# A recurrent state with an MLP behind it on one core: the order of VectorE's first work, whole first tiles, and the place of the early weights

## The chip, the cores and the metric

The kernel runs on one core of one Trainium2 chip. Its engines are TensorE (PE: matmul; PEld is its weight load), VectorE (DVE), ScalarE (ACT), GpSimd (POOL) and SyncE (SP), which issues transfers; each works through its own queue in order. The metric is the device time of one execution in microseconds (us). The median of 3 runs of the kernel before is 829.57 us.

## The reference

```python
def _attn_ref(r, k, v, w, a, b):                 # 4 x 8 heads, 768 positions, 40 wide, float32
    ...
    for t in range(S):
        ...
        y[:, :, t] = np.einsum('bhd,bhde->bhe', rt, state)
        Sa = np.einsum('bhde,bhe->bhd', state, at)
        state_decay = state * wt[:, :, None, :] - np.einsum('bhd,bhe->bhde', Sa, bt)
        state = state_decay + np.einsum('bhd,bhe->bhde', vt, kt)
...
    h = x @ w_in                                  # 3072 x 320 by 320 x 2048
    sp = np.where(h > 20.0, h, np.log1p(np.exp(np.minimum(h, 20.0))))
    g = h * np.tanh(sp)
    return (g @ w_out).astype(np.float32)         # by 2048 x 320
```

A state of 40 x 40 per head runs through 768 positions; at each position it is decayed by w, reduced by a product with a and b, and raised by v and k. The outputs y, put side by side over the heads, go through an MLP.

## The kernel before

The 768 positions are cut into 12 chunks of 64 (`C`, `nch`). Within a chunk the recurrence is solved with matrices; from chunk to chunk only the state is carried. Chunks are handled in six pairs n = 0 to 5 (chunks 2n and 2n+1). The work of a pair has three parts.

`pre_a(c, be)` (from L126) is called four times for a pair: two chunks c, two halves be of the heads. It loads a tile `wa` (decays and a, L131) and a tile `bk` (b and k, L134), two transfers each because the 40 rows of two groups of heads go to partitions 0 to 39 and 64 to 103. The first call also loads `cst` (identity and masks) and fills a column block of `bk` from it (L138). On VectorE follow a reduce (L145), two reciprocals (L146, L156), a product scan `P` forward (L147) and one backward (L157), and products into `wa` (L152) and `bk` (L170). ACT copies the scaled a to `ad` (L155). TensorE multiplies `ad` and `bk` (L186), and ACT and VectorE write the results to `GP` (L188, L189, L193) and `HA` (L190, L191); TensorE transposes `bk` (L202). `wa` and `bk` have two buffers each (`NWA`), used in turns; `P` goes to memory (L172, on GpSimd's queue).

`pre_inv(n)` (from L205) inverts triangular 32 x 32 blocks of the whole pair on VectorE: a transpose `XL` (L209), thirty times a product `tmp` (L214) and an addition (L216), each needing the one before, and two transposes `TT` and `T1` (L218, L220). `post_inv(n)` takes these on TensorE (L232, L241, L258) and ACT (L235, L249 to L251, L260) to the tiles `KT`, one for each chunk and half.

`step(c)` (from L349) runs one chunk with its state: its matmuls are L284, L293, L304, L314, L334 and L339, VectorE masks the result (L316) and forms the new state `ST` (L342, L346), ACT copies (L286, L294, L343). Step c needs the `KT` of its chunk and the state after step c - 1. GpSimd's queue carries its loads (L267 to L271) and the store of y.

The MLP (from L550) runs over the 12 chunks with weights that are split into a high and a low part by `split` (L489): a transfer `cv_d` (L453, on SP), ACT (L459, L494) and four operations of VectorE (L461 to L463, L495). `M.early()` converts the first quarter of `w_in` in three pieces with one buffer for `cv_d`; the rest follows when the space of `pre_a` is free (`M.first`, `M.second`, `M.third`).

A planner orders the instructions: each engine's queue takes, in the planner's own model of time, the ready instruction of the best priority. Priority is the place in the program, and `at(tc, k)` moves a block ahead by `OFF[k]` places (L38, L44). The program's order is `pa(0)`, `inv(0)`, the four calls of pair 1, `M.early()`, and then for each n the letters of `ORDER`: step 2n, `pa(n+2)`, `inv(n+1)`, step 2n+1.

Of the kernel before, what the change touches and what calls it, by code (L numbers as in the profile page):

```python
# [33 lines left out]
NSTN = 1  # L34
LA = 2
ORDER = '0aiA1'

OFF = {'I': 80, 'T1': 80, 'P00': -40, 'P10': 80, 'P11': 40, 'b0': 15, 'c0': 600, 'u0': -15, 'u1': 250, 'd0': 250,  # L38
       'd1': 150, 'W': 600, 'V': 400, 'E': 150, 'I0': 600, 'I1': 300, 'I2': 300, 'I3': 300, 'I4': 300, 'p4': 15,
       'I5': 300, 'J5': 600, 's0': 150, 's2': -15, 's3': 80, 's4': 250, 's6': -15, 's7': -40, 's8': 150, 's10': -150}  # L40
SORD = 'a0 b0 u0 d0 a1 b1 u1 d1 c0 c1'

# [5 lines left out]
def layouts(inp, S=768):  # L48
    nch = S // C

    def v(x):
        return x[:, :, :S].reshape(4, 2, 2, 2, nch, C, 40)

    r, k, vv, w, a, b = (v(inp[n]) for n in 'rkvwab')
    o = {}
    wt = w.transpose(4, 2, 1, 6, 3, 0, 5).reshape(nch, 2, 2, 40, 8, C)
    wa = np.zeros(wt.shape[:4] + (1040,), np.float32)
    wa[..., :520].reshape(wt.shape[:4] + (8, 65))[..., 1:] = wt
    wa[..., 528:] = a.transpose(4, 2, 1, 6, 3, 0, 5).reshape(nch, 2, 2, 40, 512)
    o['wa'] = wa  # L60
    bt, kt = (x.transpose(4, 2, 1, 6, 3, 0, 5).reshape(nch, 2, 2, 40, 8, 1, C) for x in (b, k))
    bk = np.concatenate([bt, kt], -2)
    bk[:, 1] = np.concatenate([kt, bt], -2)[:, 1]
    o['bk'] = bk.reshape(nch, 2, 2, 40, 8, 128)
    o['rD'] = np.ascontiguousarray(r.transpose(4, 1, 6, 2, 3, 0, 5)).reshape(nch, 2, 40, 16, C)
    o['vD'] = np.ascontiguousarray(vv.transpose(4, 1, 6, 3, 0, 2, 5)).reshape(nch, 2, 40, 8, 128)
    o['vN'] = np.ascontiguousarray(vv.transpose(4, 2, 5, 3, 0, 1, 6)).reshape(nch, 2, C, 16, 40)
    p = np.arange(128)
    cst = np.zeros((128, 328), np.float32)
    cst[:, :128] = np.eye(128)  # L70
    cst[:, 128:192] = (p[:, None] % 64) < np.arange(64)
    cst[:, 192:256] = np.arange(64) < (p[:, None] // 64) * 32 + p[:, None] % 32
    cst[:, 256:296] = (p[:, None] % 64) == np.arange(40)
    cst[:, 296:328] = np.arange(32) < p[:, None] % 32
    o['cst'] = cst
    return o


def attention(ctx, tc, I, yD, pD, nch, M):
# [25 lines left out]
    bdT = [ci.tile([128, 8, 2, 64], F32, name=f"bdT{i}") for i in range(2)]  # L105
    z = cs.tile([128, 1], F32, name="z")
    V.memset(z, 0.0)
    for w, b in zip(wab, bkb):
        V.memset(w, 1.0)
        G.memset(b, 0.0)  # L110
    for t in [d1] + [x.rearrange("p s k a t -> p (s k a t)") for x in adb[:NAD]]:
        A.copy(t, z.broadcast_to(t.shape))
    for t in bdT:
# [6 lines left out]
    for t in VS + [UVT] + bdr[:NBR] + ST:  # L120
        G.memset(t, 0.0)

    RW, W2, HA, BKN, GP, KT = {}, {}, {}, {}, {}, {}
    LQ, SQ, OQ, PQ = (dict(S=SP, G=G, A=A)[x] for x in QS)

    def pre_a(c, be):  # L126
        n = 2 * c + be
        wa, bk, ad = wab[n % NWA], bkb[n % NWA], adb[n % 2]
        for al in range(2):
            q = slice(al * 64, al * 64 + 40)  # L130
            LQ.dma_start(out=wa[q], in_=I['wa'][c, be, al])  # L131
        for al in range(2):
            q = slice(al * 64, al * 64 + 40)
            LQ.dma_start(out=bk[q, :, 0:128], in_=I['bk'][c, be, al])  # L134
        if (c, be) == (0, 0):
            LQ.dma_start(out=cst, in_=I['cst'])
            for t in bkb:
                A.copy(t[:, :, 128:168], cst[:, 256:296].unsqueeze(1).broadcast_to([128, 8, 40]))  # L138
        wz, a = wa[:, 0:521], wa[:, 528:1040]
        P = pw.tile([128, 520], F32, name="P", bufs=NP)  # L140
        E = wa[:, 520:1040]
        w2 = pw.tile([128, 2, 8], F32, name="w2", bufs=4)
        wz3 = wz[:, 0:520].rearrange("p (s j) -> p s j", j=65)

        V.tensor_reduce(out=w2[:, 0], in_=wz3[:, :, 1:33], axis=AX.X, op=ALU.mult)  # L145
        V.reciprocal(d1[:, 64:584:65], w2[:, 0])  # L146
        V.tensor_tensor_scan(out=P, data0=wz[:, 0:520], data1=d1[:, 64:584], initial=0.0, op0=ALU.mult, op1=ALU.add)  # L147
        P3 = P.rearrange("p (s j) -> p s j", j=65)
        E3 = E.rearrange("p (s j) -> p s j", j=65)
        V.tensor_copy(w2[:, 1], P[:, 64:520:65])  # L150
        a3 = a.rearrange("p (s t) -> p s t", t=64)
        V.tensor_tensor(out=a3, in0=a3, in1=P3[:, :, 0:64], op=ALU.mult)  # L152
        for al in range(2):
            q = slice(al * 64, al * 64 + 64)
            A.copy(ad[q, :, :, al], a[q].rearrange("p (s k t) -> p s k t", k=2, t=32))  # L155
        V.reciprocal(d1[:, 64:584:65], w2[:, 1])  # L156
        V.tensor_tensor_scan(out=E[:, 0:519][:, ::-1], data0=wz[:, 2:521][:, ::-1], data1=d1[:, 1:520][:, ::-1],  # L157
                             initial=0.0, op0=ALU.mult, op1=ALU.add)
        W2[be] = w2
        if be == 1:  # L160

            RW[c] = wk.tile([128, 2, 16], F32, name="rw", bufs=4)
            pt = ps_g.tile([128, 2, 16], F32, name="pa")
            for b2 in range(2):
                for al in range(2):
                    PE.matmul(pt[b2 * 64:b2 * 64 + 64, al], ident[:, al * 64:al * 64 + 64], W2[b2].rearrange("p a b -> p (a b)"),
                              start=(al == 0), stop=True, skip_group_check=True)
            A.copy(RW[c], pt)
        bk4 = bk[:, :, 0:128].rearrange("p s (x t) -> p s x t", x=2)
        V.tensor_tensor(out=bk4, in0=bk4, in1=E3[:, :, 0:64].unsqueeze(2).broadcast_to([128, 8, 2, 64]), op=ALU.mult)  # L170
        for al in range(2):
            PQ.dma_start(out=pD[c, be, :, al], in_=P[al * 64:al * 64 + 40])  # L172

        if c % 2 == 0 and be == 0:
            GP[c // 2] = iw.tile([128, 32, 2, 32], F32, name="GP", bufs=NGP)
        gp = GP[c // 2]
        u0 = (c % 2) * 16 + be * 8
        ha = iw.tile([128, 8, 104], F32, name="HA", bufs=NHA)
        HA[c, be] = ha
        oa, oh = (0, 40) if be == 0 else (64, 0)  # L180
        og, ok = (0, 64) if be == 0 else (64, 0)
        for s0 in (0, 3, 6):
            m = min(3, 8 - s0)
            pt = ps_g.tile([128, 3, 168], F32, name="pa")
            for j in range(m):
                PE.matmul(pt[:, j], ad[:, s0 + j].rearrange("p k a t -> p (k a t)"), bk[:, s0 + j], start=(j == 0), stop=True,  # L186
                          skip_group_check=True)
            A.mul(gp[0:64, u0 + s0:u0 + s0 + m, 1], pt[0:64, 0:m, og:og + 32], -1.0)  # L188
            A.mul(gp[64:128, u0 + s0:u0 + s0 + m].rearrange("p u k i -> p u (k i)"), pt[64:128, 0:m, og:og + 64], -1.0)  # L189
            A.copy(ha[:, s0:s0 + m, oa:oa + 40], pt[:, 0:m, 128:168])  # L190
            V.tensor_tensor(out=ha[:, s0:s0 + m, oh:oh + 64], in0=pt[:, 0:m, ok:ok + 64],  # L191
                            in1=maskH.unsqueeze(1).broadcast_to([128, m, 64]), op=ALU.mult)
        V.tensor_tensor(out=gp[:, u0:u0 + 8, 1], in0=gp[:, u0:u0 + 8, 1], in1=maskG.unsqueeze(1).broadcast_to([128, 8, 32]),  # L193
                        op=ALU.mult)

        bkn = wk.tile([128, 664], F32, name="bkn", bufs=NBKN)
        BKN[c, be] = bkn
        G.memset(bkn[:, 640:664], 0.0)
        for s0 in (0, 4):
            pt = ps_g.tile([128, 4, 2, 64], F32, name="pa")  # L200
            for j in range(4):
                PE.transpose(pt[:, j].rearrange("p a b -> p (a b)"), bk[:, s0 + j, 0:128], ident)  # L202
            A.copy(bkn[:, s0 * 80:s0 * 80 + 320].rearrange("p (s a e) -> p s a e", a=2, e=40), pt[:, :, :, 0:40])

    def pre_inv(n):  # L205
# [11 lines left out]
        TT = iw.tile([128, 32, 32], F32, name="TT", bufs=NTT)  # L217
        V.transpose(TT.rearrange("p u t -> p t u"), X)  # L218
        T1 = gp[0:64, :, 0]
        V.transpose(T1, TT[0:64])  # L220
        return TT, T1

    def post_inv(n, TT, T1):
        gp = GP[n]
# [155 lines left out]

    def inv(n):
        with at(tc, 'I%d' % n), at(tc, 'I'):
            TT, T1 = pre_inv(n)
        with at(tc, 'J%d' % n):
            post_inv(n, TT, T1)

    pa(0)
    inv(0)
    for u in range(4):
        with at(tc, 'P%d%d' % (u // 2, u % 2)):  # L390
            pre_a(2 + u // 2, u % 2)
    for n in range(nds):
        if n + 1 == nds:
            ictx.close()
            with at(tc, 'V'):
                M.second()
        if n == 0:
            with at(tc, 'E'):
                M.early()
        for k in ORDER:  # L400
            if k in '01':
                step(2 * n + int(k))
            elif k == 'i':
                if n + 1 < nds:
                    inv(n + 1)
            elif k == 'a':
                pa(n + LA)
            elif k == 'A' and n + 2 == nds:
# [249 lines left out]
```

## Time and profile before

| | us |
|---|---|
| median of 3 runs | 829.57 (829.17 to 835.69) |
| profiled execution | 826.83 |
| its span | 825.1 |
| mean granted TensorE clock | 0.964 |

The profile is that of one execution; its span is counted from its first to its last instruction. A row of the timeline has the start, the length (us), the engine, the line, the operation, what it writes and reads with the shapes, the count, and in brackets the idle time of the engine before it with what ended it. A row of a group has a count, then the busy time in us, the mean of one in ns, and the idle time before. The rows themselves stand in the prediction.

### The profile page before, as it was taken

What the parts mean: (1) busy time and instruction counts of PE and PEld (TensorE: products, weight loads), DVE (VectorE), ACT (ScalarE), POOL (GpSimd) and SP (SyncE); (2) the same over time, 40 slices, a digit from 0 to 9 for tenths busy, and PEclk for the clock granted to TensorE, in tenths of its full rate; (3) what the DMA queues carried; (4) which work ended last, traced back from release to release, by engine and by line L of the source; (5) the groups of instructions that cost most, each with busy time, mean ns of one, the idle gap of its engine ahead of it and who ended that gap; (6) DMA issues with size and microseconds to landing.
All of it is one profiled execution on the core that took longest, in us unless ns stands there. A gap on an engine that the chain in (4) does not pass through costs nothing.

```text
span 825.1 us, 18795 instructions
## 1 busy us (share of the span) xinstructions
PE 724.1 (88%) x7816; PEld 679.3 (82%) x7816; DVE 461.1 (56%) x975; ACT 428.6 (52%) x937; POOL 103.2 (13%) x182
## 2 busy tenths in 40 slices
PE   2544798999789889889886999999999999999998
PEld 1433687788788788778775899999999999999998
DVE  6789979748989758889846456222222122122110
ACT  5534658775485866666784556233333333333331
POOL 8100021223222023221102100000000000000000
PEclk9767889999989999999999999999999999999999
DMA  6522323334433233423328543121121112000000
GB/s 174 143 73 65 96 54 73 93 82 111 106 84 81 60 97 103 92 74 111 105 92 191 130 139 99 39 56 33 23 55 37 36 39 55 18 20 17 17 1 33
DMA packets 58213, 61.92 MB, mean 75 GB/s; under 512 B 25536, under 2 KB 48704, under 8 KB 58128
## 3 DMA queue, kind: packets, MB, share of 16 engines
q1 hardware_dynamic: 49296, 40.94, 17.7%
q0 software_dynamic: 8832, 19.79, 9.9%
q8 instruction: 61, 1.00, 0.5%
q14 instruction: 24, 0.20, 0.1%
HBM read 48.79 MB, written 11.86 MB: 74 GB/s over the span
## 4 chain that ended last, share of the span: by engine, by line
PE 51%; ACT 9%; DVE 8%; DMA 4%; issue 2%; SPq 0%; DVEq 0%; ACTq 0%
PE ph L583 21%; PE po L604 7%; PE po L605 7%; PE po L603 7%; PE pa L258 3%; DMA cv_d<-in_wo 2%; PE pa L186 2%; DVE tmp L214 1%; DVE XL L216 1%; ACT bdT L249 1%; ACT bdT L250 1%; PE pq L314 1%; ACT KT L260 1%; PE pu L284 1%; DMA cv_d<-in_wi 1%
## 5 line engine op out<-in xcount | busy, mean ns | idle before, releaser
L583 PE MATMUL ph<-xh,w_ih 128*128 128x256 f32 x576 | 148.3, 283 | 3.1 <-ACT xh L566 3.1
L585 ACT ACTIVATE g<-ph 128x512 f32<-128x512 f32 x96 | 57.3, 598 | 180.0 <-PE ph L583 179.9
L589 DVE TENSOR_TENSOR gl<-g,gh 128x1024 fp32r<-128x1024 f32 x48 | 58.6, 1225 | 159.1 <-ACT gh L588 158.8
L583 PE MATMUL ph<-xh,w_il 128*128 128x256 f32 x576 | 123.7, 283 | 0.0
L186 PE MATMUL pa<-bk,ad 128*128 128x168 f32 x384 | 80.6, 359 | 45.5 <-DVE bk L170 15.0
L604 PE MATMUL po<-w_ol,gh 128*128 128x320 f32 x384 | 118.7, 309 | 0.1
L605 PE MATMUL po<-w_oh,gl 128*128 128x320 f32 x384 | 118.4, 309 | 0.0
L603 PE MATMUL po<-w_oh,gh 128*128 128x320 f32 x384 | 117.9, 309 | 0.0
L583 PEld LDWEIGHTS ph<-xh,w_ih 128*128 128x128 f32 x576 | 109.3, 190 | 3.4 <-ACT xh L566 3.4
L186 PEld LDWEIGHTS pa<-bk,ad 128*128 128x128 f32 x384 | 67.0, 222 | 50.8 <-issue 22.8
L583 PE MATMUL ph<-xl,w_ih 128*128 128x256 f32 x384 | 100.9, 284 | 0.0
L583 PEld LDWEIGHTS ph<-xh,w_il 128*128 128x128 f32 x576 | 96.2, 190 | 0.1
L583 PEld LDWEIGHTS ph<-xl,w_ih 128*128 128x128 f32 x384 | 73.1, 190 | 0.5 <-issue 0.3
L604 PEld LDWEIGHTS po<-w_ol,gh 128*128 128x128 f32 x384 | 72.1, 188 | 0.5 <-DVE w_ol L495 0.5
L605 PEld LDWEIGHTS po<-w_oh,gl 128*128 128x128 f32 x384 | 72.1, 188 | 0.1
L603 PEld LDWEIGHTS po<-w_oh,gh 128*128 128x128 f32 x384 | 71.8, 188 | 0.2
L216 DVE TENSOR_TENSOR XL<-XL,tmp 128x30 f32<-128x30 f32 (+9 forms) x180 | 59.0, 328 | 2.4
L214 DVE TENSOR_TENSOR tmp<-XL 128x30 f32<-128x30 f32 (+9 forms) x180 | 58.6, 325 | 2.3
L258 PE MATMUL pa<-bdT,HA 128*104 128x128 f32 x384 | 52.3, 291 | 6.9 <-ACT bdT L251 5.7
L258 PEld LDWEIGHTS pa<-bdT,HA 128*104 128x104 f32 x384 | 47.3, 182 | 10.6 <-ACT bdT L251 7.4
L314 PE MATMUL pq<-bdr,UVT 128*128 128x128 f32 x384 | 53.7, 285 | 0.3 <-DVE UVQ L316 0.2
L588 ACT CAST gh<-g 128x1024 fp32r<-128x1024 f32 x48 | 50.1, 1048 | 1.1
(89 smaller groups left out, 1219.6 us busy)
## 6 DMA issues: line engine op xcount, KB each, us to landing
wa<-in_wa SPq DMA_DIRECT2D x48, 162.5 KB
bk<-in_bk SPq DMA_DIRECT2D x48, 160.0 KB
cv_d<-in_wi SPq DMA_DIRECT2D x12, 512.0 KB
cv_d<-in_wo SPq DMA_DIRECT2D x8, 640.0 KB
pD<-P POOLq DMA_DIRECT2D x48, 81.2 KB, 2.2
VS<-in_vN POOLq DMA_DIRECT2D x24, 160.0 KB, 3.5
UVT<-in_vD POOLq DMA_DIRECT2D x24, 160.0 KB, 4.4
bdr<-in_rD POOLq DMA_DIRECT2D x24, 160.0 KB, 4.4
```

The costliest lines, as they stand in the source:

```text
L186: PE.matmul(pt[:, j], ad[:, s0 + j].rearrange("p k a t -> p (k a t)"), bk[:, s0 + j], start=(j == 0), stop=True, skip_group_check=True)
L214: V.tensor_tensor(out=tv, in0=X[:, i + 1:32, i:i + 1].broadcast_to([128, 31 - i, i]), in1=X[:, i:i + 1, 0:i].broadcast_to([128, 31 - i, i] ...
L216: V.tensor_tensor(out=X[:, i + 1:32, 0:i], in0=X[:, i + 1:32, 0:i], in1=tv, op=ALU.add)
L258: PE.matmul(pk[:, j], ha[:, s0 + j], bd[:, s0 + j].rearrange("p a t -> p (a t)"), start=(j == 0), stop=True, skip_group_check=True)
L314: PE.matmul(pq[:, s], UVT[:, g * 4 + s, be * 128:be * 128 + 128], br[:, be, g * 4 + s].rearrange("p a t -> p (a t)"), start=(s == 0), stop ...
L583: PE.matmul(o, w, x, start=(j == 0 and n == 0), stop=(n == 7), skip_group_check=True)
L585: A.activation(g[:, f0:f0 + 2], ph, AF.Mish)
L588: A.copy(gh, g)
L589: V.tensor_tensor(out=gl, in0=g, in1=gh.bitcast(F32), op=ALU.subtract)
L603: PE.matmul(po[k], gh[:, j, t], oh, start=(f == 0), stop=False, skip_group_check=True)
L604: PE.matmul(po[k], gh[:, j, t], ol, start=False, stop=False, skip_group_check=True)
L605: PE.matmul(po[k], gl[:, j, t], oh, start=False, stop=(f == 15), skip_group_check=True)
```

## The change

The change has four parts.

1. The calls of pair 1's `pre_a` are put under `tc.issue_after(ends[0])`, where `ends[0]` is the last transpose (`T1`) of inverse 0. This gives every VectorE instruction of those calls a place in VectorE's queue behind that transpose; it is an order within one queue and no semaphore. Their offset becomes 100 (key `F`) for all four; it was -40, 0, 80 and 40.
2. For n = 0 the order of the letters is `ORDER0`: step 0, inverse 1, step 1, then `pa(2)`. The other n keep `ORDER`.
3. For chunk 0 the host lays out whole tiles of 128 partitions, `wap` (ones where there is no data) and `bkp` (zeros, and the column block that L138 copied from `cst`). The two calls for chunk 0 load them with one transfer for `wa` and one for `bk`. The memsets of the `wa` and `bk` buffers (L109, L110) and ACT's copies (L138) go.
4. `M.early()` moves from n = 0 to n = 2 (`NE`). Its VectorE instructions are ordered behind the last transpose of inverse 1 (`ends[1]`), its transfers on SP behind the last `bk` load of pair 1 (`ld`).

```diff
+ORDER0 = '0i1a'
+NE = 2
...
+       'd1': 150, 'W': 600, 'V': 400, 'E': 150, 'I0': 600, 'I1': 300, 'F': 100, 'I2': 300, 'I3': 300, 'I4': 300, 'p4': 15,
...
+    wap = np.ones((2, 2, 64, 1040), np.float32)
+    wap[:, :, 0:40] = wa[0]
+    bkp = np.zeros((2, 2, 64, 8, 168), np.float32)
+    bkp[:, :, 0:40, :, 0:128] = o['bk'][0]
+    bkp[:, :, :, :, 128:168] = np.eye(64, 40, dtype=np.float32)[:, None]
+    o['wap'] = wap.reshape(2, 128, 1040)
+    o['bkp'] = bkp.reshape(2, 128, 1344)
...
-    for w, b in zip(wab, bkb):
-        V.memset(w, 1.0)
-        G.memset(b, 0.0)
...
+        if c == 0:
+            LQ.dma_start(out=wa, in_=I['wap'][be])
+            LQ.dma_start(out=bk.rearrange("p s t -> p (s t)"), in_=I['bkp'][be])
+        else:
...
+                last[0] = LQ.dma_start(out=bk[q, :, 0:128], in_=I['bk'][c, be, al]).ins
         if (c, be) == (0, 0):
             LQ.dma_start(out=cst, in_=I['cst'])
-            for t in bkb:
-                A.copy(t[:, :, 128:168], cst[:, 256:296].unsqueeze(1).broadcast_to([128, 8, 40]))
...
-        V.transpose(T1, TT[0:64])
-        return TT, T1
+        return TT, T1, V.transpose(T1, TT[0:64])
...
     pa(0)
-    inv(0)
+
+    ends = [inv(0)]
     for u in range(4):
-        with at(tc, 'P%d%d' % (u // 2, u % 2)):
+        with at(tc, 'F'), tc.issue_after(ends[0]):
             pre_a(2 + u // 2, u % 2)
+    ld = last[0]
     for n in range(nds):
...
-        if n == 0:
-            with at(tc, 'E'):
+        if n == NE:
+            with at(tc, 'E'), tc.issue_after(ends[1]), tc.issue_after(ld):
                 M.early()
-        for k in ORDER:
+        for k in ORDER if n else ORDER0:
...
-                    inv(n + 1)
+                    ends.append(inv(n + 1))
```

More of the change, by code (lines that the diff above doesn't have):

```diff
@@ L36 @@
 ORDER = '0aiA1'
+ORDER0 = '0i1a'
+NE = 2
 OFF = {'I': 80, 'T1': 80, 'P00': -40, 'P10': 80, 'P11': 40, 'b0': 15, 'c0': 600, 'u0': -15, 'u1': 250, 'd0': 250,
-       'd1': 150, 'W': 600, 'V': 400, 'E': 150, 'I0': 600, 'I1': 300, 'I2': 300, 'I3': 300, 'I4': 300, 'p4': 15,
+       'd1': 150, 'W': 600, 'V': 400, 'E': 150, 'I0': 600, 'I1': 300, 'F': 100, 'I2': 300, 'I3': 300, 'I4': 300, 'p4': 15,
        'I5': 300, 'J5': 600, 's0': 150, 's2': -15, 's3': 80, 's4': 250, 's6': -15, 's7': -40, 's8': 150, 's10': -150}
@@ L121, in attention @@
         G.memset(t, 0.0)
+    last = [None]
     RW, W2, HA, BKN, GP, KT = {}, {}, {}, {}, {}, {}
@@ L128, in pre_a @@
         wa, bk, ad = wab[n % NWA], bkb[n % NWA], adb[n % 2]
[L129 to L134, printed above, removed]
+        if c == 0:
+            LQ.dma_start(out=wa, in_=I['wap'][be])
+            LQ.dma_start(out=bk.rearrange("p s t -> p (s t)"), in_=I['bkp'][be])
+        else:
+            for al in range(2):
+                q = slice(al * 64, al * 64 + 40)
+                LQ.dma_start(out=wa[q], in_=I['wa'][c, be, al])
+            for al in range(2):
+                q = slice(al * 64, al * 64 + 40)
+                last[0] = LQ.dma_start(out=bk[q, :, 0:128], in_=I['bk'][c, be, al]).ins
         if (c, be) == (0, 0):
             LQ.dma_start(out=cst, in_=I['cst'])
-            for t in bkb:
-                A.copy(t[:, :, 128:168], cst[:, 256:296].unsqueeze(1).broadcast_to([128, 8, 40]))
         wz, a = wa[:, 0:521], wa[:, 528:1040]
@@ L382, in inv @@
         with at(tc, 'I%d' % n), at(tc, 'I'):
-            TT, T1 = pre_inv(n)
+            TT, T1, end = pre_inv(n)
         with at(tc, 'J%d' % n):
             post_inv(n, TT, T1)
+        return end.ins
     pa(0)
-    inv(0)
+    ends = [inv(0)]
     for u in range(4):
-        with at(tc, 'P%d%d' % (u // 2, u % 2)):
+        with at(tc, 'F'), tc.issue_after(ends[0]):
             pre_a(2 + u // 2, u % 2)
+    ld = last[0]
     for n in range(nds):
```

## The prediction

> **What bounds the kernel now.** I read the page first: the engines' rows and the 40 slices.
>
> ```profile
> PE 724.1 (88%) x7816; PEld 679.3 (82%) x7816; DVE 461.1 (56%) x975; ACT 428.6 (52%) x937; POOL 103.2 (13%) x182
> PE   2544798999789889889886999999999999999998
> DVE  6789979748989758889846456222222122122110
> ```
>
> TensorE (PE) is full from the 23rd slice on (22 x 20.6 = 454 us): that is the MLP. What a change at the beginning can win is how much earlier that stretch begins. TensorE's holes lie in the first five slices, where VectorE (DVE) carries the high digits. The windows view gives this by stage; its columns are stage, length, then busy us and instructions of PE, PEld, DVE, ACT, POOL, then granted clock, DMA share, GB/s:
>
> ```profile
> 0.00:25.00 25.00, 7.87 (x45) 7.00 (x45) 17.86 (x33) 12.80 (x29) 17.57 (x29) 1.00 0.67 170
> 25.00:50.00 25.00, 14.12 (x68) 11.82 (x68) 18.35 (x37) 12.98 (x38) 1.97 (x8) 0.73 0.37 113
> 48.00:97.00 49.00, 22.59 (x181) 18.04 (x180) 48.18 (x120) 21.73 (x63) 5.07 (x10) 0.79 0.24 71
> 97.00:147.00 50.00, 45.78 (x598) 41.45 (x599) 42.94 (x110) 32.93 (x83) 9.97 (x18) 0.90 0.32 76
> 147.00:178.00 31.00, 28.15 (x510) 24.71 (x508) 14.77 (x33) 24.77 (x65) 6.05 (x11) 1.00 0.38 84
> 200.00:250.00 50.00, 43.00 (x545) 38.58 (x545) 43.16 (x108) 33.46 (x88) 10.67 (x21) 0.90 0.38 102
> 250.00:300.00 50.00, 44.88 (x755) 39.76 (x754) 37.95 (x89) 37.41 (x97) 8.88 (x17) 1.00 0.26 71
> 300.00:350.00 50.00, 45.21 (x544) 40.31 (x545) 39.48 (x105) 30.90 (x86) 14.55 (x26) 1.00 0.41 101
> 350.00:400.00 50.00, 42.81 (x724) 38.60 (x723) 43.51 (x115) 34.96 (x86) 9.94 (x16) 0.97 0.36 101
> ```
>
> From 48 to 97 us VectorE has 0.8 us free and bounds; TensorE idles 26 of 49. From 97 on TensorE is 91% busy and bounds (73.9 of 81 us), VectorE even rests for 16 of 31 us from 147 to 178. The third view is VectorE's timeline:
>
> ```profile
> 48.23 2.10 DVE L209 STREAM_TRANSPOSE XL<-GP 128x1024 f32<-128x1024 f32 x1
> 55.19 1.23 DVE L147 TENSOR_TENSOR_SCAN P<-wa,d 128x520 f32<-128x520 f32 x1
> 56.34 0.27 DVE L214 TENSOR_TENSOR tmp<-XL 128x130 f32<-128x130 f32 x1
> 76.83 0.40 DVE L214 TENSOR_TENSOR tmp<-XL 128x234 f32<-128x234 f32 x1
> 77.26 0.40 DVE L216 TENSOR_TENSOR XL<-XL,tmp 128x234 f32<-128x234 f32 x1
> 92.58 1.94 DVE L218 STREAM_TRANSPOSE TT<-XL 128x1024 f32<-128x1024 f32 x1
> 94.57 1.22 DVE L220 STREAM_TRANSPOSE GP<-TT 64x1024 f32<-64x1024 f32 x1
> 97.15 2.10 DVE L209 STREAM_TRANSPOSE XL<-GP 128x1024 f32<-128x1024 f32 x1
> 143.44 1.96 DVE L218 STREAM_TRANSPOSE TT<-XL 128x1024 f32<-128x1024 f32 x1
> 178.24 2.15 DVE L209 STREAM_TRANSPOSE XL<-GP 128x1024 f32<-128x1024 f32 x1
> L216 DVE TENSOR_TENSOR XL<-XL,tmp 128x30 f32<-128x30 f32 (+9 forms) x180 | 59.0, 328 | 2.4
> L214 DVE TENSOR_TENSOR tmp<-XL 128x30 f32<-128x30 f32 (+9 forms) x180 | 58.6, 325 | 2.3
> ```
>
> Inverse 0 runs from 48.2 to 94.5 us, inverse 1 from 97.2 to 145.4, inverse 2 begins at 178.2. Between an inverse's operations stand those of `pre_a` (such as the scan at 55.19). So the first pair's steps, TensorE's first large work, wait for 94.5.
>
> **The change, part by part.**
>
> *Start.* VectorE's first load of use is the reduce at 7.76; ahead of it stand a memset of wa and a weight piece:
>
> ```profile
> 1.06 0.93 DVE L109 MEMSET wa<- 128x1040 f32 x1 [0.19 <-issue]
> 7.76 0.41 DVE L145 TENSOR_REDUCE w<-wa 128x8 f32<-128x256 f32 x1
> 9.60 0.67 DVE L495 SCALAR_TENSOR_TENSOR w_il<-cv_w,w_ih 128x512 fp32r<-128x512 f32 x1
> 14.78 0.41 DVE L145 TENSOR_REDUCE w<-wa 128x8 f32<-128x256 f32 x1
> 26.11 0.43 DVE L461 TENSOR_SCALAR cv_w<-cv_m 128x512 int32<-128x512 int32 x1
> 27.27 0.69 DVE L462 SCALAR_TENSOR_TENSOR cv_w<-cv_m,cv_w 128x512 int32<-128x512 int32 x1
> 27.99 0.69 DVE L463 SCALAR_TENSOR_TENSOR cv_w<-cv_d,cv_w 128x512 int32<-128x512 int32 x1
> 31.01 0.69 DVE L495 SCALAR_TENSOR_TENSOR w_il<-cv_w,w_ih 128x512 fp32r<-128x512 f32 x1
> 0.00:2.50 2.50, 0.00 (x0) 0.00 (x0) 1.34 (x3) 1.76 (x2) 1.97 (x6) 1.00 0.29 72
> 2.50:5.00 2.50, 0.00 (x0) 0.00 (x0) 0.57 (x1) 2.50 (x5) 2.50 (x4) 1.00 0.86 278
> 5.00:7.50 2.50, 0.00 (x0) 0.00 (x0) 1.52 (x3) 0.88 (x2) 2.50 (x3) 1.00 0.69 221
> ```
>
> The padded wa is 128 x 1040 x 4 = 532 KB. Transfers move from about 2 us on (72 GB/s until 2.5, then 278), so 532 KB take 1.9 us: landed near 4.5 us, no earlier than 4, and no later than 6.4 if the first bk (688 KB) shares the engines with it. I take 4.5, since the queue issues wa first: 3.3 us won (1.4 to 3.8). In all the four padded tiles carry 1.15 MB more than before, 4 us at 278 GB/s; the second wa is wanted at 4.5 + 14.78 - 7.76 - 0.6 = 11 us, and with the first wa and bk and cst (164 KB) ahead it is 1.92 MB in all, landed at 8.9: covered. The two memsets of bk on POOL, the two of wa and ACT's two column copies go: POOL and ACT have room there, nothing on the path. SP issues four transfers fewer.
>
> *Early weights.* A piece costs VectorE 0.43 + 0.69 + 0.69 + 0.69 = 2.5 us. In the first pair's way lie the operation at 9.60 and the piece from 26.11 to 31.01 (part of that beside a wait): 2.9 us. The third piece lies in a wait at 42 to 47 us and is worth nothing there. All 7.5 us come back later; from 200 to 400 us VectorE is busy 164 of 200, so 36 free us cover them: cost 0 (0 to 7.5). On SP a piece's transfer waits for the one buffer, with wa and bk loads queued behind; bounds 0 and one call of `pre_a` (5.8 us, below); I take 0: among all waits of the first 100 us none is VectorE's on a transfer.
>
> So inverse 0 may begin at 48.2 - 3.3 - 2.9 = 42.0.
>
> *Inverse 0 alone.* Its operations: (59.0 + 58.6) / 6 = 19.6 us, and transposes 2.1 + 1.9 + 1.2 = 5.2. Dependent neighbours stand 0.03 us apart beyond their length (76.83 and 77.26: 0.43 for a 0.40); independent ones overlap 0.08 (55.19 to 56.34: 1.15 for a 1.23). Alone it takes 19.6 + 60 x 0.03 + 5.2 = 26.6, so TT stands at 42.0 + 25.4 = 67.4 instead of 94.5: 27 us sooner for the steps. Interleaving had been cheaper by 60 x 0.11 = 6.6 us of VectorE. The Trainium skill ("VectorE: DVE Perf Modes", The DRAIN you can't avoid) says that the next operation doesn't start until the pipe is empty, so that breaking chains wins nothing; by that rule the 6.6 us would be 0 and the result 6.6 us lower. The rows disagree, 1.15 start to start after a 1.23, and the sum goes by the rows.
>
> *What is late next.* The second pair's four calls, which ran inside inverse 0, now come after it. Between 48 and 97 VectorE's 48.2 us less the inverse's 20 (26.6 - 6.6) leave 28 for nearly five calls: 5.8 us each, 23.4 a pair. Step 0 comes beside them:
>
> ```profile
> L316 DVE TENSOR_TENSOR UVQ<-pq,cst 128x512 f32<-128x512 f32 x48 | 33.0, 687 | 11.5 <-PE pq L314 11.4
> L342 DVE TENSOR_TENSOR stn<-ST,pq 128x160 f32<-128x160 f32 x44 | 13.9, 315 | 14.5 <-PE pq L339 13.8 <-PE pq L334 0.4
> L346 DVE TENSOR_TENSOR ST<-stn,R 128x320 f32<-128x320 f32 x22 | 10.6, 481 | 0.0
> ```
>
> 4 x 0.687 + 4 x 0.315 + 2 x 0.481 = 5.0 us a step. With 9.7 us idle (below) inverse 1 starts at 42.0 + 26.6 + 23.4 + 5.0 + 9.7 = 107, not 97. It keeps fillers: nothing orders pair three behind it. Step 1 now comes ahead of pair three's calls; both lie in the equal work below, so I take 0, between a loss of one call (5.8) and the 16 us that VectorE rested from 147 to 178 behind step 1's products.
>
> *The sum.* The work of 48 to 178 us is the same in both kernels, so I lay it out anew from 42.0. VectorE: 48.2 + 42.9 + 14.8 = 105.9, plus 6.6, ends at 154.5 without idle time. Idle time: the only other stretch in which one pair's calls ran without an inverse to fill it is 7.76 to 48; the two first windows leave 13.8 us idle, 4.1 of it before 7.76 (the three short rows have 3.4 busy): 9.7. Taken once for the second pair, plus 4 beside inverse 1 (97 to 147 had 7): 168. Bounds: 154.5 and, with nothing gained, 178. TensorE: idle until 67.4, then 22.6 + 45.8 + 28.2 = 96.5, ends at 164 if never idle, and 168 if the 91% hold for half of it (48.2 + 48.2 / 0.91). Both give 178 - 168 = 10 us.
>
> TensorE's idle 25 us cool it, too:
>
> ```profile
> 30.00:35.00 5.00, 3.70 (x13) 3.65 (x14) 2.75 (x6) 0.83 (x3) 0.00 (x0) 0.50 0.72 223
> 55.00:60.00 5.00, 0.81 (x3) 0.84 (x4) 5.00 (x12) 1.23 (x2) 1.01 (x2) 0.50 0.16 39
> ```
>
> After rests the granted clock is 0.50. The work of 48 to 97 ran at 0.79 and would mostly run at 1.0 in the new place, which wins back some 22.6 x 0.2 = 4 us, against at most 2.5 lost at 67 (such a stage of 5 us at half the clock): taken as 0, since both lie within the bounds above. The skill ("TensorE: Matmul & The Clock Gate", The HAM clock gate) speaks against the change here: about 3.4 us idle halve the clock until as much busy time has passed, an estimate of 1.7 us lost after the rest at 67; the trace agrees on the 0.50.
>
> Against the profiled execution (826.83 us, span 825.1) this is 816.8. The median shown is 829.57, 2.7 above it; I predict 829.6 - 10 = about 819.
>
> **Rivals.**
>
> *Given back later (827).* From 200 to 400 us neither engine is full (VectorE 82%, TensorE 88%): what orders those stages are the places in in-order queues, which the same offsets now set from another beginning. For it: the rest at 147 to 178 shows that such a hole costs as much as the whole gain. Against: 10 us more of finished work must be lost again. Little is left then: 827.
>
> *Slower (841).* After 67.4 the second pair's calls share ACT and TensorE with `post_inv(0)` and step 0, and VectorE stands in order before each HA read. In 147 to 178, where steps and calls met like this, VectorE was busy only 14.8 of 31 (48%). At that share the 28.4 us of calls and step 0 take 59, not 38 (28.4 + 9.7): 21 more, 829.6 - 10 + 21 = 841. It decides from the point where inverse 1 starts after about 117. Against: 97 to 147 met the same mixture with 86%.
>
> *All of it (806).* VectorE without idle time: 178 - 154.5 = 23.7 us, 806. For it: 48 to 97 ran that full. Against: without inverse 0's operations as fillers it had 9.7 idle.
>
> *It doesn't do what it says (829).* Other work could still fill inverse 0. Against: pair three's buffers (two wa) aren't free before the second pair's calls.
>
> **How the numbers follow.** Forecast 0.42 (own range 808 to 828: 0.34 faster, 0.08 same), given back 0.22, slower 0.16, all of it 0.16, no effect 0.04. Faster by over 1% (under 821; 1% is about what a measurement of this kernel can tell): 0.34 + 0.16 = 0.50; same 0.08 + 0.22 + 0.04 = 0.34; slower 0.16. The range 803 to 834 leaves out most of the slower case and the lowest few.
>
> **What would show it.** The first reduce near 4.5; inverse 0's transposes at 42 and 65, with no `pre_a` operation between; first KT soon after 70; inverse 1 from about 107; inverse 2 near 168; weight pieces outside the first 100 us; TensorE full from about 444. I am wrong if inverse 1 starts after 117, if VectorE idles over 14 us between 67 and 168, or if inverse 2 comes at 168 and TensorE is still full only from 454.

## The result and the profile after

| | before | after |
|---|---|---|
| median | 832.63 us (4 runs) | 845.13 us (4 runs, 844.87 to 846.28) |
| ratio to before, 95% interval | 1 | 1.0134 (1.0091 to 1.0177) |
| profiled execution, its span | 826.83, 825.1 us | 845.0, 843.2 us |

The change makes the kernel 1.3% slower; a time near 819 us was forecast. In the changed kernel the lines of the attention stand 9 or 10 further down: L201 is L191 of before (HA), L196 is L186, L219 is L209 (`XL`), L230 is L220 (`T1`), L351 and L355 are L342 and L346. First the page of the changed kernel, engines and slices:

```profile
PE 736.7 (87%) x7816; PEld 688.3 (82%) x7816; DVE 464.4 (55%) x973; ACT 427.9 (51%) x935; POOL 101.0 (12%) x180
PE   3705985789999889898888999999999999999998
DVE  6587669889979846978954539221222222122110
PEclk9665999789999989989998999999999999999999
```

The third slice of TensorE has become a 0: that is inverse 0 alone. Then its timeline on VectorE:

```profile
4.40 0.42 DVE L155 TENSOR_REDUCE w<-wa 128x8 f32<-128x256 f32 x1 [3.53 <-DMA wa<-in_wap]
43.79 2.09 DVE L219 STREAM_TRANSPOSE XL<-GP 128x1024 f32<-128x1024 f32 x1
69.82 1.24 DVE L230 STREAM_TRANSPOSE GP<-TT 64x1024 f32<-64x1024 f32 x1
106.60 1.24 DVE L167 TENSOR_TENSOR_SCAN wa<-wa,d 128x519 f32<-128x519 f32 x1 [2.20 <-ACT ad L165]
113.13 0.36 DVE L201 TENSOR_TENSOR HA<-pa,cst 128x192 f32<-128x192 f32 x1 [2.74 <-ACT HA L200]
122.23 2.13 DVE L219 STREAM_TRANSPOSE XL<-GP 128x1024 f32<-128x1024 f32 x1
169.35 1.24 DVE L230 STREAM_TRANSPOSE GP<-TT 64x1024 f32<-64x1024 f32 x1
```

The beginning is as forecast: the first reduce at 4.40 (4.5 in the prediction), inverse 0 from 43.8 (42.0), alone in 27.3 us to 71.1 (26.6). From there it isn't. The second pair's four calls take from 71.1 to 122.2, 51 us, and inverse 1 ends at 170.6; before it ended at 146.7. The windows view shows the two stages, first of the changed kernel, then of the kernel before:

```profile
44.00:70.00 26.00, 0.74 (x10) 0.50 (x12) 23.83 (x64) 0.93 (x3) 0.00 (x0) 0.59 0.04 13
70.00:123.00 53.00, 46.68 (x640) 40.89 (x638) 34.08 (x68) 38.86 (x104) 10.75 (x20) 0.88 0.33 86
123.00:170.00 47.00, 31.74 (x324) 27.59 (x324) 43.89 (x114) 22.89 (x64) 9.01 (x16) 0.85 0.37 101
```

```profile
44.00:70.00 26.00, 11.28 (x58) 9.31 (x56) 23.86 (x59) 11.54 (x33) 3.04 (x6) 0.76 0.28 81
70.00:123.00 53.00, 39.74 (x478) 34.67 (x480) 47.30 (x120) 26.78 (x71) 7.56 (x13) 0.81 0.24 66
123.00:170.00 47.00, 40.90 (x679) 36.08 (x676) 34.46 (x84) 37.59 (x97) 8.02 (x16) 1.00 0.39 89
```

From 70 to 123 us VectorE rests 53 - 34.1 = 18.9 us, and TensorE and ACT are fuller than before; from 123 to 170 it is the other way round, VectorE has 43.9 of 47 and TensorE rests 15.3. The work that TensorE can do after inverse 0 (its matmuls, steps 0 and 1) is used up at 143; what it gets next, the matmuls of the third pair's calls and those behind inverse 1, hangs on VectorE. One place shows how. TensorE's timeline, and VectorE's operation that it waits for:

```profile
139.60 1.41 PE L196 MATMUL pa<-bk,ad 128*128 128x168 f32 x8
149.25 1.73 PE L212 MATMUL pa<-cst,bk 128*128 128x128 f32 x7 [8.25 <-DVE HA L201]
```

```profile
147.92 0.40 DVE L224 TENSOR_TENSOR tmp<-XL 128x240 f32<-128x240 f32 x1
148.24 0.20 DVE L166 RECIPROCAL d<-w 128x8 f32<-128x8 f32 x1
148.35 0.41 DVE L226 TENSOR_TENSOR XL<-XL,tmp 128x240 f32<-128x240 f32 x1
148.75 0.35 DVE L201 TENSOR_TENSOR HA<-pa,cst 128x192 f32<-128x192 f32 x1
```

The matmuls for HA ended at 141.0; VectorE read them only at 148.75, since in its queue the read stands behind operations of inverse 1 and of another call. TensorE stood 8.25 us.

The lag is there to stay. The new state `ST` is written twice a step; the second writes of steps 1 to 4, after and then before:

```profile
142.56 0.48 DVE L355 TENSOR_TENSOR ST<-stn,R 128x320 f32<-128x320 f32 x1
208.64 0.48 DVE L355 TENSOR_TENSOR ST<-stn,R 128x320 f32<-128x320 f32 x1
242.89 0.49 DVE L355 TENSOR_TENSOR ST<-stn,R 128x320 f32<-128x320 f32 x1
271.39 0.48 DVE L355 TENSOR_TENSOR ST<-stn,R 128x320 f32<-128x320 f32 x1
```

```profile
173.93 0.48 DVE L346 TENSOR_TENSOR ST<-stn,R 128x320 f32<-128x320 f32 x1
198.93 0.48 DVE L346 TENSOR_TENSOR ST<-stn,R 128x320 f32<-128x320 f32 x1
228.44 0.45 DVE L346 TENSOR_TENSOR ST<-stn,R 128x320 f32<-128x320 f32 x1
261.15 0.49 DVE L346 TENSOR_TENSOR ST<-stn,R 128x320 f32<-128x320 f32 x1
```

Step 1 is 31 us ahead, but then nothing can follow: step 2 needs inverse 1. It ends 10 us behind, step 3 14 us behind, step 4 10. From step 4 to the end of the span the changed kernel takes 571.8 us and the kernel before 563.9; the windows view of the two stretches, after and then before:

```profile
271.39:843.20 571.81, 541.08 (x5394) 517.90 (x5392) 245.79 (x456) 274.07 (x536) 42.07 (x70) 0.98 0.25 65
```

```profile
261.15:825.10 563.95, 531.04 (x5418) 509.58 (x5410) 245.23 (x452) 273.87 (x536) 42.09 (x70) 1.00 0.24 66
```

TensorE has nearly the same number of matmuls there, and rests even less in the changed kernel (30.7 us against 32.9); but it is busy 10 us longer, at a granted clock of 0.98 against 1.00. So of the 18.1 us between the two spans 10.2 are lost ahead of step 4, and the 7.9 behind it are not idle time but go with the clock. A fairer pair is the changed kernel and e1 below, which is as fast as the kernel before: its profile has nearly the changed kernel's clock (0.947 against 0.941), TensorE is busy 736.6 us in the one and 736.7 in the other, and the 11.0 us between the spans are idle time of TensorE (95.6 us in e1, 106.5 in the changed kernel).

### The profile page after: what moved, and what is told of

It reads as the page before. It is cut to its first block, busy times and chain, and to the rows that moved or that the text cites. A ratio compares the mean times of both kernels' runs of the same rounds, so it can differ in the third digit from the quotient of the medians.

```text
span 843.2 us, 18782 instructions
## 1 busy us (share of the span) xinstructions
PE 736.7 (87%) x7816; PEld 688.3 (82%) x7816; DVE 464.4 (55%) x973; ACT 427.9 (51%) x935; POOL 101.0 (12%) x180
## 4 chain that ended last, share of the span: by engine, by line
PE 60%; DVE 16%; ACT 13%; issue 5%; DMA 5%; SPq 1%; DVEq 0%; ACTq 0%
PE ph L595 20%; PE po L616 7%; PE po L617 7%; PE po L615 7%; PE pa L196 4%; PE pa L267 4%; DVE tmp L224 3%; DVE XL L226 3%; PE pq L323 3%; DMA cv_d<-in_wo 2%; PE pq L343 2%; PE pa L212 2%; DMA cv_d<-in_wi 1%; PE pu L293 1%; ACT GP L199 1%
## 5 line engine op out<-in xcount | busy, mean ns | idle before, releaser
L595 PE MATMUL ph<-xh,w_ih 128*128 128x256 f32 x576 | 148.3, 283 | 1.0 <-ACT xh L578 1.0
L196 PE MATMUL pa<-bk,ad 128*128 128x168 f32 x384 | 79.7, 355 | 19.2 <-DVE bk L180 11.3
L196 PEld LDWEIGHTS pa<-bk,ad 128*128 128x128 f32 x384 | 66.0, 219 | 24.4 <-issue 15.9
L267 PE MATMUL pa<-bdT,HA 128*104 128x128 f32 x384 | 55.4, 302 | 6.4 <-ACT bdT L260 4.5
L267 PEld LDWEIGHTS pa<-bdT,HA 128*104 128x104 f32 x384 | 50.2, 191 | 10.1 <-ACT bdT L260 6.8
L212 PE MATMUL pa<-cst,bk 128*128 128x128 f32 x192 | 35.2, 304 | 20.3 <-DVE HA L201 14.5
```

The costliest lines, as they stand in the source:

```text
L267: PE.matmul(pk[:, j], ha[:, s0 + j], bd[:, s0 + j].rearrange("p a t -> p (a t)"), start=(j == 0), stop=True, skip_group_check=True)
L595: PE.matmul(o, w, x, start=(j == 0 and n == 0), stop=(n == 7), skip_group_check=True)
```

## The experiments

The first theory was that the change loses because inverse 1 ends 24 us later. Against it stood two others: that the early weights in their new place (170 to 204 us) cost the time, and that any edit throws the planner's order by 10 us either way. Ratios are to the kernel before on the same chip, with 95% intervals; they are estimates over all runs and differ by up to 0.4% from the quotients of the medians. All experiments but the first four build on what came out of them. The table gathers, from the profile of each, the first transpose of inverse 1 and its last, the starts of the second write of `ST` in steps 3 and 4, with which the step ends, and the span (us).

| kernel | order behind inverse 0 | offset | letters at n = 0 | inverse 1 from, last | step 3 | step 4 | span | ratio |
|---|---|---|---|---|---|---|---|---|
| before | no | old | old | 97.2, 145.5 | 228.4 | 261.2 | 825.1 | 1 |
| changed | yes | 100 | new | 122.2, 169.4 | 242.9 | 271.4 | 843.2 | 1.0134 |
| e1 whole tiles only | no | old | old | 98.7, 145.9 | 234.7 | 267.3 | 832.2 | 1.0011 |
| e2 tiles, early weights | no | old | old | 96.6, 136.6 | 228.3 | 263.5 | 834.7 | 0.9986 |
| e3 | yes | 600 | new | 109.7, 161.9 | 238.5 | 266.3 | 832.4 | 1.0010 |
| e4 third pair behind inverse 1 | yes | 100 | new | 119.3, 148.3 | 258.5 | 286.2 | 859.5 | 1.0263 |
| e5 early weights at n = 0 | yes | 100 | new | 125.6, 174.0 | 257.7 | 287.2 | 852.9 | 1.0253 |
| e6 early weights at n = 3 | yes | 100 | new | 122.2, 169.3 | 242.3 | 274.9 | 844.6 | 1.0173 |
| e7 | yes | 100 | old | 121.0, 174.1 | 248.2 | 274.9 | 846.4 | 1.0154 |
| e8 | yes | 600 | old | 109.7, 163.3 | 231.3 | 258.7 | 827.8 | 0.9927 |
| e9 | no | 600 | old | 97.6, 136.2 | 226.5 | 258.3 | 828.2 | 0.9866 |
| e10 | yes | 300 | old | 110.5, 162.1 | 236.2 | 264.4 | 834.2 | 0.9979 |
| e11 early weights at n = 0 | yes | 600 | old | 114.9, 168.3 | 236.7 | 265.3 | 837.1 | 0.9961 |
| e12 old loads | yes | 600 | old | 113.0, 167.1 | 236.0 | 263.4 | 830.4 | 0.9899 |
| e13 | no | 100 | old | 97.3, 135.8 | 224.6 | 257.5 | 828.0 | 0.9964 |
| e14 | yes | old | old | 128.3, 181.9 | 248.9 | 277.5 | 848.7 | 1.0232 |
| e15 as e8 | yes | 600 | old | 108.6, 161.8 | 229.2 | 256.6 | 825.5 | 0.9964 |
| e16 as e9 | no | 600 | old | 98.1, 137.2 | 226.9 | 259.7 | 830.2 | 0.9955 |

From the end of step 4 to the end of the span every one takes 563.9 to 573.3 us, while step 4 itself ends anywhere from 257 to 287: most of what separates the spans arises ahead of step 4. Over the eighteen profiles the end of step 4 and the span go together with a correlation of 0.97.

### Parts alone, and what brings inverse 1 forward

**e1_tiles**, only the whole tiles; order, letters and early weights as before:

```diff
-ORDER0 = '0i1a'
-NE = 2
+ORDER0 = ORDER
+NE = 0
...
-        with at(tc, 'F'), tc.issue_after(ends[0]):
+        with at(tc, 'P%d%d' % (u // 2, u % 2)):
...
-            with at(tc, 'E'), tc.issue_after(ends[1]), tc.issue_after(ld):
+            with at(tc, 'E'):
```

> Part 3 alone (whole first tiles); order, letters and early weights as before. Late-inverse theory (the change lost because inverse 1 ends 24 us later): first reduce near 4.4 us, inverse 1 ends at about 142 us or sooner, time 0.995 to 1.000 of before. Weights theory (the early pieces in their new place, 170 to 203 us, cost the time): the same, 0.995 to 1.000. Chance theory (any edit gives the planner another order, worth 10 us either way): anywhere from 0.985 to 1.015.

Measured: 836.33 us against 833.52, 1.0011 (0.9977 to 1.0045). Whole tiles alone give nothing that can be measured. The first reduce comes at 4.45, but inverse 1 ends where it did (147.1; 142 or sooner was expected).

**e2_tiles_early**, as e1, but the early weights at n = 2 with their orders, as in the change.

> Parts 3 and 4 (whole tiles, early weights at the third pair), without the order behind inverse 0 and with the old letters. Late-inverse theory: inverse 1 ends before 140 us, time 0.985 to 0.997 of before. Weights theory: slower, 1.005 to 1.015, with the loss after the pieces. Chance theory: anywhere from 0.985 to 1.015, without regard to the end of inverse 1.

Measured: 833.2, 0.9986 (0.9955 to 1.0018). The weights theory expected a loss and there is none; inverse 1 ends 9 us sooner than before, yet step 2 ends at 200.0, as before (198.9). The first theory's range (0.985 to 0.997) lies under the measured ratio, too, though the interval reaches into it: an earlier inverse 1 won nothing that shows here, where step 1 ends only at 175 us.

**e3_f600**:

```diff
-'F': 100
+'F': 600
```

> The changed kernel with offset 600 instead of 100 for the second pair's calls, so that they go ahead of step 0 and of the matmuls behind inverse 0 in every queue. Late-inverse theory: the calls take 30 to 40 us instead of 51, inverse 1 starts near 105 and ends near 152 us (it was 170), and at least half of the loss goes: 0.995 to 1.005 of before. Weights theory: 1.010 to 1.016, as the changed kernel. Chance theory: no relation between the end of inverse 1 and the time.

Measured: 835.78, 1.0010 (0.9981 to 1.0039). The calls take 40 us instead of 51, inverse 1 starts at 109.7, and the loss is gone. But inverse 1 ends at 163.2, not near 152: that is 16 us later than before, and the time is that of before.

**e4_rest_after**:

```diff
-                pa(n + LA)
+                with tc.issue_after(ends[1]) if n == 0 else nullcontext():
+                    pa(n + LA)
```

> The changed kernel with the third pair's VectorE operations put behind inverse 1 as well. Late-inverse theory: inverse 1 starts at about 115 to 122, runs in 30 to 33 us instead of 48 (only steps fill it), ends near 150, and steps 2 and 3 come 15 to 20 us sooner; but inverse 2, whose calls now come after, ends 10 to 20 us later than 227: 0.995 to 1.015 of before. Weights theory: 1.010 to 1.016 or more. Chance theory: no relation.

Measured: 858.75, 1.0263 (1.0205 to 1.0321). Inverse 1 does run in 30 us and ends at 149.6, as the first theory had it; but step 2 ends no sooner (212.2) and step 3 at 258.5, later still, where 15 to 20 us sooner was expected. The third pair's calls now stand behind inverse 1 as the second pair's stand behind inverse 0, and they take as long: 50.9 us from the end of inverse 1 to the start of inverse 2 (149.6 to 200.5, weight pieces among them), 15.7 of them idle on VectorE. Why step 2 is no sooner was not taken apart. The end of inverse 1 by itself does not set the time: the first theory was too narrow. It took a better one: the calls of the second pair share TensorE and ACT with the matmuls behind inverse 0 and with step 0, and what VectorE loses there has to be made up ahead of step 4, wherever it is put.

### Weights and letters

**e5_early_n0** (`NE = 0`, its two orders left out), **e6_early_n3** (`NE = 3`), **e7_old_letters** (`ORDER0 = ORDER`), each a single edit of the changed kernel, and **e8_f600_old_letters** with offset 600 and `ORDER0 = ORDER`.

> The changed kernel with the early weights back at their old place (n = 0, no order behind inverse 1). Sharing theory (the second pair's calls take 51 us because they share ACT and TensorE with the matmuls behind inverse 0 and with step 0, so inverse 1 starts at 122 and steps 2 and 3 come 10 to 14 us late): inverse 1 starts at 118 or later, 1.008 to 1.020 of before. Weights theory (the pieces at 170 to 204 us lie between inverse 1 and step 2 and cost the time): step 2 ends near 200, 0.995 to 1.003.

Measured: 855.65 against 834.72, 1.0253 (1.0220 to 1.0285): worse than the changed kernel. Inverse 1 starts at 125.6, after 118 as the sharing theory had it, but the loss lies beyond that theory's upper end (1.020); the weights theory expected none.

> The changed kernel with the early weights one pair later (n = 3). Sharing theory: inverse 1 as in the changed kernel (122 to 170 us), steps 2 and 3 within 3 us of it (209 and 243), 1.009 to 1.016 of before. Weights theory: step 2 ends 5 to 8 us sooner, near 202, and the time is 1.000 to 1.006.

Measured: 848.89, 1.0173 (1.0134 to 1.0212), at the sharing theory's upper end (1.016). Steps 2 and 3 end where they did (208.6 and 242.3). The weights theory has fallen with these two.

> The changed kernel with the old letters at n = 0: pair three's calls and inverse 1 ahead of step 1. Sharing theory: inverse 1 still starts after 115, 1.005 to 1.018 of before. Letters theory (step 1, done at 143 us, leaves TensorE without work until inverse 1 ends at 170): step 1 runs later, TensorE's idle time from 100 to 200 us falls from 22 us to under 14, and the time is 0.997 to 1.005.

Measured: 847.56, 1.0154 (1.0121 to 1.0187). Step 1 does run later (163 us instead of 143), but TensorE's idle time from 100 to 200 us is 25 us (22 in the changed kernel): the letters theory fails at offset 100.

> Offset 600 for the second pair's calls and the old letters at n = 0. Sharing theory: inverse 1 starts near 110 as with offset 600 alone, time within 3 us of that run (0.997 to 1.004 of before). Letters theory: step 1 fills TensorE behind inverse 1's start, and the time is 3 to 8 us under that run: 0.990 to 0.997.

Measured: 829.24, 0.9927 (0.9902 to 0.9953): faster than the kernel before, and by more than the sharing theory allowed. With the calls in front, the old letters seem to pay, 6.5 us against e3; but the same kernel, measured again as e15, has 0.9964, whose interval overlaps that of e3, so this gain is not settled. The stage that the sharing theory is about, as the windows view of this kernel has it:

```profile
70.00:123.00 53.00, 45.22 (x578) 40.04 (x573) 40.57 (x91) 38.92 (x104) 11.87 (x22) 0.89 0.43 107
123.00:170.00 47.00, 37.50 (x464) 33.13 (x463) 44.56 (x117) 30.11 (x85) 9.80 (x18) 0.86 0.36 98
```

TensorE and ACT are as busy from 70 to 123 as in the changed kernel (46.7 and 38.9), but VectorE gets 40.6 us done instead of 34.1, and TensorE then has 37.5 instead of 31.7. Who waited on VectorE in this stage, from the list of waits (total us, times, longest), in the changed kernel and in e8:

```profile
DVE HA L201 <- ACT HA L200: 6.9, 5, 2.7
DVE wa L167 <- ACT ad L165: 4.7, 3, 2.2
DVE UVQ L325 <- PE pq L323: 2.3, 3, 1.4
DVE stn L351 <- PE pq L343: 2.0, 3, 1.0
```

```profile
DVE wa L167 <- ACT ad L165: 7.6, 4, 3.7
DVE HA L201 <- ACT HA L200: 4.1, 3, 2.7
```

With offset 100 VectorE stood 4.3 us for step 0's own products, too (UVQ, stn). With 600 step 0 comes behind the calls (it ends at 117.7), where inverse 1 fills VectorE, and these waits are gone. All waits of the stage together are 18.4 us with 100 and 12.1 with 600, although the one for `ad` (L167) is longer with 600.

### What the parts are worth with the calls in front

**e9_no_order** (e8 without `tc.issue_after(ends[0])`), **e10_f300** (offset 300), **e11_early_n0** (`NE = 0`, its two orders left out), **e12_old_loads** (old loads, memsets and copies), each a single edit of e8.

> Offset 600 and old letters, but nothing ordered behind inverse 0 (parts 3 and 4 stay). If the order is what pays in the faster kernel: the calls of the second pair stand inside inverse 0 again, it ends near 90 us instead of 70, and the time goes back to 0.998 to 1.003 of before. Rival (the offset alone pays, the order nothing): 0.989 to 0.995.

Measured: 828.96 against 839.22, 0.9866 (0.9819 to 0.9913). The calls stand inside inverse 0 again, which ends at 97.7; the time does not go back. It lies even under the rival's range (0.989 to 0.995); the rival had the direction: the order is not what pays.

> Offset 300 between the 100 of the change and the 600, old letters. Sharing theory: the time follows the start of inverse 1 (110 us with 600, 121 with 100): with a start at 112 to 117 it is 0.995 to 1.008 of before. Chance theory: no relation, for instance 1.010 and more with a start at 112, or under 0.990.

Measured: 836.13, 0.9979 (0.9951 to 1.0007), inside what the sharing theory expected, though inverse 1 started at 110.5, as with 600, and not between.

> Offset 600 and old letters, with the early weights at their old place. By the prediction's term (2.9 us on the first pair's way, 7.5 us of VectorE in all): inverse 0 starts 2 to 4 us later than 42.8, time 0.995 to 1.001 of before. Rival (from the run with the old place and offset 100, which lost 10 us against the changed kernel): 1.002 to 1.010.

Measured: 835.59, 0.9961 (0.9934 to 0.9988). Inverse 0 starts at 44.9, 2.1 us later than in e8; its interval overlaps that of e8 (0.9902 to 0.9953), so where the early weights stand is not told apart here.

> Offset 600 and old letters, with the old loads, memsets and copies. By the prediction's term (3.3 us at the start): the first reduce comes 1 to 3.5 us later than 4.4 us, and the time is 0.994 to 0.999 of before. Rival (a start 3 us sooner is lost on the way, as in the run with whole tiles alone): 0.990 to 0.994.

Measured: 831.71, 0.9899 (0.9869 to 0.9929). The first reduce comes at 7.99, 3.6 us later, and the time shows nothing of it: the rival, at its lower edge.

### Order or offset

Order and offset had come together in the change. Two runs fill the missing cells of a table, and two put order and no order at offset 600 side by side on one chip. **e13_offset100_no_order** and **e14_old_offsets_order** differ from e7 in one of the two edits of this line, **e15_f600_order** is e8, **e16_f600_no_order** is e9:

```diff
-        with at(tc, 'F'), tc.issue_after(ends[0]):
+        with at(tc, 'F'):
...
-        with at(tc, 'F'), tc.issue_after(ends[0]):
+        with at(tc, 'P%d%d' % (u // 2, u % 2)), tc.issue_after(ends[0]):
```

> Whole tiles, early weights at the third pair, old letters, offset 100 for the second pair's calls, and no order behind inverse 0: one cell of a table order x offset. If the order is what costs (its partner with the order and the same offset was 1.015): 0.985 to 1.000, the calls stand inside inverse 0, which ends near 95 us, and inverse 1 ends near 137. If the offset 100 costs by itself: 1.008 to 1.018.

> The same cell with the order, but the old offsets (-40, 0, 80, 40) of the second pair's calls. If the order costs wherever the calls don't go ahead of the first pair's steps: 1.012 to 1.025, inverse 1 starts after 120 us. If the offset 100 costs by itself: 0.995 to 1.003.

> Offset 600, old letters, with the order (as in the run before that was 0.993), beside the next kernel on one chip. If the order pays at offset 600: at least 0.4% under the next one. If it costs there too: 0.2 to 1.0% over it.

> Offset 600, old letters, without the order (0.987 before, on another chip). If the order pays at offset 600: 0.995 to 1.000 of before here. If the order costs there too: 0.983 to 0.992, and under the kernel beside it.

Measured, with e2 and e7 (all with whole tiles, early weights at n = 2 and old letters):

| offset of the second pair's calls | no order | order behind inverse 0 |
|---|---|---|
| old (-40, 0, 80, 40) | 0.9986 (0.9955 to 1.0018) | 1.0232 (1.0174 to 1.0291) |
| 100 | 0.9964 (0.9928 to 1.0001) | 1.0154 (1.0121 to 1.0187) |
| 600, one chip | 0.9955 (0.9922 to 0.9988) | 0.9964 (0.9933 to 0.9994) |

In the left column the offset does not matter. In the right one it decides: the order costs 2.5% with the old offsets, 1.9% at 100 and nothing at 600. e13 and e14 came as a cost of the order had it; at 600 neither branch of the expectation did, since the order neither pays nor costs there. The sizes are rougher than the intervals say: e2 and e7 ran on another chip than e13 and e14, and two kernels measured on two chips each have ratios 0.4% and 0.9% apart (e8 and e15: 0.9927 and 0.9964; e9 and e16: 0.9866 and 0.9955). The costs of 2.5% and 1.9% are larger than that.

With the order the calls take 128.3 - 69.1 = 59 us with the old offsets, 51 at 100 and 40 at 600. So the order is what costs, and it costs where the offset leaves the calls late. Nor does chance explain it: every kernel without the order lies at 0.987 to 1.001, every one with it at offset 300 or 600 at 0.990 to 1.001, and every one with it at 100 or the old offsets at 1.013 to 1.026. The reading that fits is that the order holds back VectorE's instructions of the calls, while the places of the other queues leave the first pair's work ahead of them. With or without the order, offset 600 is about 0.4% faster than the kernel before, by the ratios. None of these runs separates that gain from what tiles and early weights give.

## Why the prediction was wrong

*Right.* The start (4.40 against 4.5), the start of inverse 0 (43.8 against 42.0) and its length alone (27.3 against 26.6). That its operations, set in a chain, cost about 7 us of VectorE holds: neighbours stand 0.28 us apart for a 0.24 in the changed kernel, too. The Trainium skill's page "VectorE: DVE Perf Modes" (The DRAIN you can't avoid), by whose rule the prediction worked out 0 for this term beside its own 6.6, says in the same paragraph that "a next op that is not held starts earlier". The trace has such earlier starts: 1.15 us after the start of a 1.23 in the prediction's rows. That the early weights are covered later was right for their first stretch: e2 is not slower, and with the order they were better late (e5). The four whole tiles carry 1.12 MB more, not 1.15, which changes nothing in the sum.

*The step that failed: "9.7. Taken once for the second pair, plus 4 beside inverse 1".* The 4 was right (3.1 from 123 to 170). The 9.7 us of idle time were 18.9 from 70 to 123. They were taken from the first pair's calls, which had no step and no matmuls behind an inverse beside them. The second pair's calls, pushed behind inverse 0, meet the matmuls behind it and step 0, and ran 51 us instead of 38; the rest of the difference is work, 32.3 us on VectorE where the sum had 28.4. With offset 600 the calls take 40 us, 12.1 of them idle in e8, with step 0 behind them, and the loss is gone: so this term was mis-sized.

*The premise that failed with it: "The work of 48 to 178 us is the same in both kernels".* The sum was made to the start of inverse 2. That came at 175.8, even 2.4 us ahead of before, and the kernel is slower all the same. By then TensorE had only begun the matmuls behind inverse 1 (169.4 to 194.1), which ran from 149.1 to 172.1 before; the early weights had just begun (170.8 to 203.9), and the fourth pair's second call was still to come. A milestone that reads well on VectorE said little of the steps that wait for inverse 1. e8 and e15 show it from the other side: inverse 2 starts at 164.5 and 163.0, 14 and 15 us ahead of before, but step 4 is only 2.5 and 4.5 us ahead, and the time 0.7% and 0.4% less. So the 10 us would not have come with the right idle time either, much as the rival "given back later" had it. Step 4 would have been the better point: over the eighteen profiles its end goes with the span (correlation 0.97), the start of inverse 2 much less (0.60), though behind step 4 the profiles still differ by up to 9.4 us.

*The signs.* Two of those that the prediction had named came: inverse 1 started after 117, and VectorE idled 22.2 us between 67 and 168, more than 14.

*The rivals.* The slower one named this mechanism and its point ("from the point where inverse 1 starts after about 117"): it started at 122.2. 841 was worked out, 845.13 measured, but the closeness is partly luck: the rival gave the calls and step 0 59 us where they took 51, and with 51 its own sum makes 829.6 - 10 + 13 = 833. It had 0.16 against 0.42 because 97 to 147 us, where VectorE was busy to 86%, was taken as the better likeness; there an inverse filled its gaps, which the order forbids. What was given to the early start (3.3 us) does not show at the end of the kernel (e1, e12).

*What stays open.* Why step 2 takes 38 us after inverse 1 here, and 34 in e8, was not taken apart. The order's cost is shown; that its way is the sharing of TensorE and ACT fits the waits, the cure (offset 600) and the same cost behind inverse 1 in e4, but no kernel was run in which nothing was shared.

## What to carry to other kernels

An order within one engine's queue, as it was put here, moves only that engine's work: where the same work was not also moved ahead in the other queues, it came out late, behind what was ready in the meantime. When work is moved from beside one stage to beside another, take its idle time from a stage in which the same engines are shared, not from one where it ran alone. And make the sum to a point whose place goes with the end of the span, here the end of step 4, not to the next start on the engine being ordered.

## What the runs showed of the hardware

Single executions of one kernel spread by 1.4%, and with TensorE's granted clock: on the first experiments' chip, the kernel before took 827.59 us at a mean clock of 0.963 and 838.93 at 0.941, and over its 25 runs there clock and time go together with a correlation of -0.87. The medians stand beside the kernel before on the same chip for that reason. The changed kernel's four runs lay at 0.939 to 0.945, so part of its loss may go with the clock. Over the runs this was not separated; in the profiles, 11.0 us remain against e1 at nearly the same clock, and e7 and e14 lost 1.5% and 2.3% with their profiled executions at 0.949 and 0.948.

After the rest of some 25 us, TensorE's granted clock was down as the prediction had it, at 0.50 from 50 to 75 us. TensorE started again at 69.8, and the clock was still 0.50 from 76 to 80 and 1.00 only from 84 on:

```profile
50.00:75.00 25.00, 3.02 (x106) 2.89 (x108) 22.27 (x56) 4.82 (x11) 1.01 (x2) 0.50 0.01 4
76.00:80.00 4.00, 3.31 (x15) 3.34 (x16) 3.81 (x7) 2.04 (x6) 0.74 (x2) 0.50 0.17 56
80.00:84.00 4.00, 4.00 (x32) 3.52 (x32) 1.40 (x2) 2.09 (x6) 0.27 (x1) 0.66 0.21 69
84.00:88.00 4.00, 3.20 (x26) 2.71 (x25) 3.03 (x8) 3.84 (x12) 0.00 (x0) 1.00 0.25 79
```

The prediction had taken 5 us at half the clock. From 68 to 80 TensorE was busy 7.2 us at 0.50, so that half of it, an estimate of 3.6 us, was lost there, and not 2.5 at most.
